# A maximum of three as the third plus two relus kept in PSUM, with the third's product folded into the down sums

## The chip, the cores and the metric

One core of a Trainium2 chip runs the whole program. The metric is the device time of one execution in microseconds (us), the median over several runs. The kernel before: 1981.44 us, median of 3 runs (1980.41 to 1981.76).

## What is computed

Eight batches of 3072 rows with 256 columns go through a real Fourier transform along the rows, a complex 256x256 product with bias, a soft threshold on real and imaginary part, and the inverse transform. The result, 24576 rows of 256, goes through a maxout layer: three products up to 768 columns, their maximum, and one product down to 256.

```python
X = np.fft.rfft(x, axis=1); Xr, Xi = X.real, X.imag
Yr = Xr @ w_r - Xi @ w_i + b_r
Yi = Xr @ w_i + Xi @ w_r + b_i
Yr = np.sign(Yr) * np.maximum(np.abs(Yr) - 0.01, 0.0)   # Yi likewise
y = np.fft.irfft(Yr + 1j * Yi, n=3072, axis=1)          # reshaped to 24576 x 256

h = np.maximum(np.maximum(y @ w1, y @ w2), y @ w3)      # 24576 x 768
out = h @ w_out                                         # 24576 x 256
```

## The kernel before

Products that must be accurate are made of three f16 matmuls: each operand is split into a high and a low f16 part, and `mm3` (lines 178 to 181) issues high x high, high x low and low x high into one PSUM sum. Splitting takes two instructions: ScalarE (ACT) writes the high part, VectorE (DVE) subtracts it and writes the low part (`split_later`, lines 165 to 176, the DVE half handed to `later` and issued at the next `flush`).

The program has a prologue (batch 0's transform, and the maxout weights, which come as float64 bit patterns and are put together and split on DVE and ACT) and then one long loop: batches b (8), chunks c of 384 rows (8 per batch), and units f (6 per chunk, 128 of the 768 up columns each). That makes 64 chunks and 384 units. In a unit:

- `up` (line 1047) makes three products `pu`, i = 0, 1, 2 for w1, w2, w3. Each is two `mm3` (256 = 2 x 128 rows of the weight), so 6 matmuls of 384 columns; a unit has 18. ACT copies the first into SBUF (`c1`, line 1056), DVE takes the maximum with the second in place (line 1059) and with the third into `h32` (line 1062), and `h32` is split into `hh`.
- `down` (line 1071) multiplies `hh` of a unit two units old with its 128 rows of w_out: three groups of 128 rows, each one `mm3`, so 9 matmuls of 256 columns, summed over the six units of a chunk into the two PSUM tiles `pd`. After the sixth, ACT writes them out as `o` (line 1091).

Between these steps of the loop, `run_until(pos)` issues the Fourier work of later batches at positions counted in units (the list `events`), three times per unit: at pos - 2/3, pos - 1/3 and pos. For one block k of that work the path is: `ab`, split by `split_a` and moved across partitions by four DMAs on SP's queue; `stage_b`, 16 matmuls into `px` (line 737); two ACT copies of `px` (`tt` at line 173, `s` at line 750), DVE's low part of `tt` (line 174) and its sum into `s` (line 753), ACT's and DVE's split of `s` (lines 170 and 171); then `stage_w1`, 6 matmuls into `py` that read this last split; then `stage_w2`, 12 more. `stage_w1` is placed one position, one unit, behind `stage_b`. There are 77 such blocks. Each engine takes its instructions in the order in which they stand.

The inverse transform of the next chunk (`inverse`) makes `yh` and `yl`, the split of y.

PSUM has eight banks: three tiles for `pu`, three for all Fourier work, two for `pd`.

Of the kernel before, what the change touches and what calls it, by code (L numbers as in the profile page):

```python
# [101 lines left out]
def fourier_maxout_kernel(  # L102
# [105 lines left out]
    wuh = const.tile([P, 3, KD, FF], F16, name="wuh")  # L208
    wul = const.tile([P, 3, KD, FF], F16, name="wul")
# [18 lines left out]
    def first_homes():  # L228
        g = ga_sb.bitcast(F32).rearrange("p i e n m -> p (i e n m)")
        w = wuh.bitcast(F32).rearrange("p i k f -> p (i k f)")  # L230
        homes = [quad_tile("aq"), quad_tile("aq"), quad_tile("zq")]
        homes += [g[:, i * NQ * D:(i + 1) * NQ * D] for i in range(3)]
        return homes + [w[0:96, i * NQ * D:(i + 1) * NQ * D] for i in range(2)]
# [110 lines left out]
    class Weights:  # L344
        def __init__(self, name, parts):
            self.name, self.parts, self.raw = name, parts, {}
            self.mx = fft.tile([P, len(parts)], F32, name="mw" + name, bufs=1)

        def load(self, n, homes=None):
            width = 2 * self.parts[n][0].shape[1]  # L350
# [17 lines left out]
        def scale(self):  # L368
            e = exponent_of(self.mx, self.name, 20, 0x7FF, 910.0)
            self.e = small("ew" + self.name)  # L370
            nc.vector.tensor_scalar(
                out=self.e, in0=e, scalar1=1.0, scalar2=-896.0, op0=ALU.mult, op1=ALU.add
            )
            self.sc = power("sw" + self.name, e, -1.0, 1164.0, 1)

        def phases(self, n):
            raw = self.raw[n]
            pair, width = raw.shape[1:3]
            if pair == 2:
                hi, lo = self.parts[n][4]  # L380
# [30 lines left out]
            def finish():  # L411
                split_scaled(hi, lo, m, self.sc)

            return exponent, combine, join, finish
# [5 lines left out]
        (wuh[:, i, kd, v:v + HALF], wul[:, i, kd, v:v + HALF], None,  # L420
         up_v[i][:, 2 * v:2 * v + 2 * HALF].rearrange("(k p) w -> p k w", p=P),
         [t[:, i, :, v:v + HALF] for t in (wuh, wul)])
        for v in range(0, FF, HALF) for i in range(3) for kd in range(KD)
    ])
# [6 lines left out]


# [614 lines left out]
    def up(y, f, i):  # L1047
        p = ps.tile([P, 512], F32, name="pu", tag="up", bufs=3)[:, 0:NT]
        for kd in range(KD):
            mm3(  # L1050
                p, wuh[:, i, kd, f * P:(f + 1) * P], wul[:, i, kd, f * P:(f + 1) * P],
                y[0][:, kd], y[1][:, kd], start=kd == 0, stop=kd == KD - 1,
            )
# [18 lines left out]
    def down(b, c, f, hh):  # L1072
        end = b == NB - 1 and c == NCH - 1
        if f == 0:
            st["pd"] = [ps.tile([P, 512], F32, name="pd", tag="dn", bufs=2) for _ in range(2)]
        pd = [st["pd"][t // 2][:, t % 2 * D:t % 2 * D + D] for t in range(3)]
        for t in range(3):
# [3 lines left out]
                stop=f == NF - 1 and t != 0, skip_group_check=t < 2,  # L1081
            )
        if f == NF - 1:
# [52 lines left out]
    for n in range(0, 6, 2):  # L1136
        planned(n, prepare, w_up, n)
        planned(5 + n // 2, phase, w_up, n)
# [13 lines left out]
    for k in range(-3, NJP + 1):  # L1152
        for fn, i in (
            (load_a, k + 3), (stage_b, k + 1), (stage_w, k), (finish_w, k), (stage_q, k - 1),
        ):
            if 0 <= i < NJP:
                if fn == stage_q and i == NJP - 1:
                    total = small("total")
                    nc.vector.tensor_tensor(out=total, in0=w_up.e, in1=w_dn.e, op=ALU.add)
                    st["lim", "u"] = limits("u", total, 273.0)  # L1160
# [55 lines left out]
    behind = []  # L1216
    st["slot"] = 0
    for b in range(NB):
        for c in range(NCH):
            nxt = (b, c + 1) if c + 1 < NCH else (b + 1, 0) if b + 1 < NB else None  # L1220
            for f in range(NF):
                pos = b * SLOTS + c * NF + f
                up(y, f, 0)
# [7 lines left out]
                up(y, f, 1)  # L1231
# [5 lines left out]
                hh = up(y, f, 2)  # L1237
                behind.append((b, c, f, hh))
# [6 lines left out]
                if b == c == 0:  # L1245
                    pumps(5)
                    if f == 2:
                        with tc.issue_after(quiet[0]):
                            split_fft_weights(fft_weights)
                    if f in (3, 5):  # L1250
# [9 lines left out]
            y = y_next  # L1260
    flush()
# [35 lines left out]
```

## Time and profile before

| | |
|---|---|
| median of 3 runs | 1981.44 us |
| span of the profiled execution | 1978.9 us |
| TensorE (PE) busy | 1961.3 us, 99% |
| VectorE (DVE) busy | 1521.3 us, 77% |
| ScalarE (ACT) busy | 1064.3 us, 54% |
| GpSimd (POOL) busy | 280.5 us, 14% |
| main loop starts | at about 110.8 us |

The span runs from the first to the last instruction. The profiled execution's own time is not listed beside it; the three runs stand 1.5 to 2.9 us above the span. A matmul's duration in the trace is from its start to the end of its result; the next one starts long before that, so the time that PE spends on one is the distance from start to start, not the mean duration of its row.

### The profile page before, as it was taken

What the parts mean: (1) busy time and instruction counts of PE and PEld (TensorE: products, weight loads), DVE (VectorE), ACT (ScalarE), POOL (GpSimd) and SP (SyncE); (2) the same over time, 40 slices, a digit from 0 to 9 for tenths busy, and PEclk for the clock granted to TensorE, in tenths of its full rate; (3) what the DMA queues carried; (4) which work ended last, traced back from release to release, by engine and by line L of the source; (5) the groups of instructions that cost most, each with busy time, mean ns of one, the idle gap of its engine ahead of it and who ended that gap; (6) DMA issues with size and microseconds to landing.
All of it is one profiled execution on the core that took longest, in us unless ns stands there. A gap on an engine that the chain in (4) does not pass through costs nothing.

```text
span 1978.9 us, 44328 instructions
## 1 busy us (share of the span) xinstructions
PE 1961.3 (99%) x16839; PEld 1355.9 (69%) x16839; DVE 1521.3 (77%) x3159; ACT 1064.3 (54%) x2186; POOL 280.5 (14%) x510
## 2 busy tenths in 40 slices
PE   9989999999999999999999999999999999999999
PEld 5746776676766766666766676666676677766666
DVE  3788887888877988778887888868887687765554
ACT  5755664566545565456554565545655455443343
POOL 1001111111111122111121021111122001100000
PEclk9999999999999999999999999999999999999999
DMA  8756564565545564555555465544552344221111
GB/s 291 212 150 172 157 163 124 156 174 154 145 133 163 143 189 115 151 150 161 159 137 149 133 186 145 147 139 130 149 154 73 90 115 123 68 76 49 49 49 33
DMA packets 201843, 269.75 MB, mean 136 GB/s; under 512 B 30846, under 2 KB 149982, under 8 KB 201534
## 3 DMA queue, kind: packets, MB, share of 16 engines
q1 hardware_dynamic: 168830, 191.37, 36.7%
q0 software_dynamic: 25168, 68.59, 10.7%
q10 hardware_dynamic: 7632, 6.95, 1.2%
q8 instruction: 133, 2.18, 0.5%
q14 instruction: 80, 0.66, 0.1%
HBM read 124.31 MB, written 75.50 MB: 101 GB/s over the span
## 4 chain that ended last, share of the span: by engine, by line
PE 93%; DVE 3%; DMA 2%; ACT 1%; issue 1%; SPq 0%; ACTq 0%; DVEq 0%
PE pu L179 19%; PE pu L181 18%; PE pu L180 18%; PE pd L181 6%; PE pd L180 6%; PE pd L179 6%; PE py L179 3%; PE py L180 3%; PE py L181 3%; PE pi L1021 2%; PE px L737 2%; PE pa L575 2%; PE pz L905 1%; PE pa L592 1%; PE py L692 0%
## 5 line engine op out<-in xcount | busy, mean ns | idle before, releaser
L179 PE MATMUL pu<-yh,wuh 128*128 128x384 f16 x2304 | 752.2, 327 | 2.6 <-DVE h L1062 1.7
L181 PE MATMUL pu<-yh,wul 128*128 128x384 f16 x2304 | 751.5, 326 | 0.0
L180 PE MATMUL pu<-yl,wuh 128*128 128x384 f16 x2304 | 751.5, 326 | 0.0
L173 ACT ACTIVATE hh<-h 128x384 f16<-128x384 f32 x384 | 200.2, 521 | 432.3 <-DVE h L1062 428.4
L181 PEld LDWEIGHTS <-wul 128*128 128x128 f16 x2304 | 225.5, 98 | 149.7 <-issue 0.9
L179 PEld LDWEIGHTS <-wuh 128*128 128x128 f16 x2304 | 225.3, 98 | 145.1 <-issue 34.2
L181 PE MATMUL pd<-woh,hh 128*128 128x256 f16 x1152 | 313.4, 273 | 0.7 <-DVE hh L174 0.7
L180 PE MATMUL pd<-wol,hh 128*128 128x256 f16 x1152 | 313.8, 273 | 0.0
L179 PE MATMUL pd<-woh,hh 128*128 128x256 f16 x1152 | 313.8, 273 | 0.0
L180 PEld LDWEIGHTS <-wuh 128*128 128x128 f16 x2304 | 225.5, 98 | 116.1 <-issue 5.0
L174 DVE SCALAR_TENSOR_TENSOR hh<-h,hh 128x384 f16<-128x384 f32 x384 | 213.3, 555 | 108.3 <-ACT hh L173 105.4
L1059 DVE TENSOR_TENSOR c<-pu,c 128x384 f32<-128x384 f32 x384 | 212.1, 552 | 95.8 <-PE pu L181 90.3
L1056 ACT ACTIVATE c<-pu 128x384 f32<-128x384 f32 x384 | 186.7, 486 | 139.9 <-PE pu L181 136.8
L1062 DVE TENSOR_TENSOR h<-pu,c 128x384 f32<-128x384 f32 x384 | 211.7, 551 | 29.2 <-PE pu L181 24.8
L1093 POOL DMA_DIRECT2D out_dram<-o x189 | 104.7, 559 | 581.3 <-ACT o L1091 569.7
L585 POOL DMA_DIRECT2D a_d<-aq x160 | 94.0, 591 | 612.4 <-ACT aq L582 590.0
L181 PE MATMUL py<-wch,tt 128*128 128x256 f16 x504 | 137.3, 273 | 0.0
L179 PE MATMUL py<-wch,tt 128*128 128x256 f16 x504 | 137.3, 272 | 0.0
L180 PE MATMUL py<-wcl,tt 128*128 128x256 f16 x504 | 137.3, 272 | 0.0
L179 PEld LDWEIGHTS <-hh 128*128 128x128 f16 x1152 | 112.7, 98 | 33.5
L180 PEld LDWEIGHTS <-hh 128*128 128x128 f16 x1152 | 112.7, 98 | 33.4
L181 PEld LDWEIGHTS <-hh 128*128 128x128 f16 x1152 | 112.7, 98 | 15.2 <-DVE hh L174 1.9
(236 smaller groups left out, 2659.3 us busy)
## 6 DMA issues: line engine op xcount, KB each, us to landing
zq<-z_d SPq DMA_DIRECT2D x63, 384.0 KB, 4.8
out_dram<-o POOLq DMA_DIRECT2D x189, 128.0 KB, 3.3
ab<-a_d SPq DMA_DIRECT2D x84, 256.0 KB, 4.1
ab<-ab SPq DMA_DIRECT2D x336, 64.0 KB, 3.0
vb<-vb SPq DMA_DIRECT2D x308, 64.0 KB, 2.9
z_d<-zs POOLq DMA_DIRECT2D x70, 256.0 KB, 3.8
xm<-in_x_dram SPq DMA_DIRECT2D x40, 384.0 KB, 3.5
a_d<-aq POOLq DMA_DIRECT2D x160, 96.0 KB, 2.9
```

The lines of the kernel that those rows point to most:

```text
L173: nc.scalar.activation(out=hi, in_=src, func=AF.Copy, scale=scale)
L174: later(lambda: low(nc.vector.scalar_tensor_tensor(out=lo, in0=src, scalar=scale, in1=h, op0=ALU.mult, op1=ALU.subtract)))
L179: nc.tensor.matmul(o, lh, rh, start=start, stop=False, **kw)
L180: nc.tensor.matmul(o, lh, rl, start=False, stop=False, **kw)
L181: st["mm"] = nc.tensor.matmul(o, ll, rh, start=False, stop=stop, **kw)
L575: st["mm"] = nc.tensor.matmul(pa[r][64 * h:64 * h + 64], ft[rows, t], xt[rows, i, h], start=t == i, stop=t == 1,)
L585: nc.gpsimd.dma_start(out=av[1 - r, :, :, n:n + 512], in_=o[64 * h:64 * h + 48])
L737: nc.tensor.matmul(pv[:, h, :, g // 2, g % 2], ah[:, g // 2, g % 2, h * P:(h + 1) * P], mb_sb[:, i, 4 * kb + g].rearrange("p (c m) -> p c ...
L1056: st["act"] = nc.scalar.activation(out=c1, in_=p, func=AF.Copy)
L1059: st["dve"] = nc.vector.tensor_tensor(out=c1, in0=p, in1=c1, op=ALU.max)
L1062: st["dve"] = nc.vector.tensor_tensor(out=h32, in0=p, in1=st["c1"], op=ALU.max)
L1093: q.dma_start(out=out_v[b, c, t], in_=o)
```

## The change

max(a, b, c) = c + relu((b - c) + relu(a - b)). The weights are held as W1 - W2 and W2 - W3 (`finish` subtracts the next weight before the split), so `up` has two products. The first, y(W1 - W2), goes into `pu`; ACT applies relu to it in place, in PSUM; the second, y(W2 - W3), is accumulated onto it; DVE then takes max(., 0), scaled, into `h32`. The term c, y W3, is not formed: G = W3 Wout is made once (`turn_last` transposes W3 by matmuls with the identity, `join_last` multiplies it with w_out) and y G joins the down sums: 6 matmuls of 256 columns for each group of 128 rows, at f = 0, 1, 2 of a chunk (in the first chunk all at f = 5). The second product of a unit is issued one unit later, behind the first product of the next unit, and `down` follows that.

```diff
-    wuh = const.tile([P, 3, KD, FF], F16, name="wuh")
+    wuh = const.tile([P, 2, KD, FF], F16, name="wuh")
+    wth = const.tile([P, NF, D], F16, name="wth")
+    gh = const.tile([P, KD, D], F16, name="gh")
...
             def finish():
+                if self.less:
+                    other = self.raw[n + 2][:, :, :, 1].bitcast(F32)
+                    nc.vector.tensor_tensor(out=m, in0=m, in1=other, op=ALU.subtract)
                 split_scaled(hi, lo, m, self.sc)
...
+    def turn_last(n):
+        m = w_up.raw[n][:, :, :, 1].bitcast(F32)
+        first = (n // 6) * (NF // 2)
+        for fs in ((0, 1), (2,)):
+            pt = ff_tile("pw").rearrange("p (f c) -> p f c", c=D)
+            for i, f in enumerate(fs):
+                for kd in range(KD):
+                    nc.tensor.matmul(
+                        pt[:, i, kd * P:(kd + 1) * P], m[:, kd, f * P:(f + 1) * P], id_sb, start=True, stop=True
+                    )
+            to = slice(first + fs[0], first + fs[-1] + 1)
+            split_scaled(wth[:, to], wtl[:, to], pt[:, 0:len(fs)], w_up.sc)
+
+    def join_last():
+        pg = ff_tile("pg").rearrange("p (k d) -> p k d", k=KD)
+        for kd in range(KD):
+            for f in range(NF):
+                mm3(
+                    pg[:, kd], *(t[:, f, kd * P:(kd + 1) * P] for t in (wth, wtl)), woh[:, f], wol[:, f],
+                    start=f == 0, stop=f == NF - 1,
+                )
+        split_scaled(gh, gl, pg, H_SCALE)
...
-    def up(y, f, i):
-        p = ps.tile([P, 512], F32, name="pu", tag="up", bufs=3)[:, 0:NT]
+    def up(y, f, i, p=None):
+        if i == 0:
+            p = ps.tile([P, 512], F32, name="pu", tag="up", bufs=3)[:, 0:NT]
...
         if i == 0:
-            st["c1"] = c1 = ffn.tile([P, NT], F32, name="c1")
-            st["act"] = nc.scalar.activation(out=c1, in_=p, func=AF.Copy)
-        elif i == 1:
-            c1 = st["c1"]
-            st["dve"] = nc.vector.tensor_tensor(out=c1, in0=p, in1=c1, op=ALU.max)
-        else:
-            h32 = ffn.tile([P, NT], F32, name="h32")
-            st["dve"] = nc.vector.tensor_tensor(out=h32, in0=p, in1=st["c1"], op=ALU.max)
-            hh = ffn.tile([P, 2, NT], F16, name="hh", bufs=4)
-            split_later(hh[:, 0], hh[:, 1], h32, H_SCALE)
-            return hh
+            st["act"] = nc.scalar.activation(out=p, in_=p, func=AF.Relu)
+            return p
+        h32 = ffn.tile([P, NT], F32, name="h32")
+        st["dve"] = nc.vector.tensor_scalar(
+            out=h32, in0=p, scalar1=0.0, scalar2=H_SCALE, op0=ALU.max, op1=ALU.mult
+        )
+        hh = ffn.tile([P, 2, NT], F16, name="hh", bufs=4)
+        split_later(hh[:, 0], hh[:, 1], h32)
+        return hh
...
+        for t in range(3):
+            if f == (NF - 1 if first else t):
+                for kd in range(KD):
+                    mm3(
+                        pd[t], *(v[:, kd, t * P:(t + 1) * P] for v in y), gh[:, kd], gl[:, kd],
+                        start=False, stop=first and kd == KD - 1 and t != 0, skip_group_check=t < 2,
+                    )
...
+    def second():
+        b, c, f, y, p = open_unit
+        behind.append((b, c, f, y, up(y, f, 1, p)))
...
-                up(y, f, 0)
+                unit = b, c, f, y, up(y, f, 0)
                 flush()
...
                 run_until(pos - 2 / 3)
-                up(y, f, 1)
+                if open_unit:
+                    second()
+                open_unit = unit
                 flush()
...
-                hh = up(y, f, 2)
-                behind.append((b, c, f, hh))
                 if len(behind) > 2:
                     down(*behind.pop(0))
```

What that does to the order of the engines is shown at three places; the names in the rows are those of the tiles above, and lines are those of the kernel that the row belongs to.

On TensorE, in the middle of the program, the end of a `down` of one of a chunk's first three units and what follows it now:

```order
L181 MATMUL pd<-woh,hh 128x256
L179 LDWEIGHTS yh
L179 MATMUL pd<-gh,yh 128x256
L180 LDWEIGHTS yh
L180 MATMUL pd<-gl,yh 128x256
L181 LDWEIGHTS yl
L181 MATMUL pd<-gh,yl 128x256
```

Before, the next product of `up` stood right behind the row of line 181; now six of these matmuls (two times the three shown) come between in half of the units, and no third product of `up` comes at all.

On VectorE, around one block's split of `px` and of its sum `s` (the 40th of the 77), before:

```order
L174 SCALAR_TENSOR_TENSOR tt<-px,tt 128x2x256
L753 SCALAR_TENSOR_TENSOR s<-px,s 128x256
L1062 TENSOR_TENSOR h_13480<-pu,c_13433 128x384
L171 TENSOR_TENSOR tt<-s,tt 128x2x128
L174 SCALAR_TENSOR_TENSOR hh<-h_13480,hh 128x384
```

and now:

```order
L174 SCALAR_TENSOR_TENSOR tt<-px,tt 128x2x256
L1089 TENSOR_SCALAR h_12377<-pu 128x384
L783 SCALAR_TENSOR_TENSOR s<-px,s 128x256
L171 TENSOR_TENSOR hh<-h_12377,hh 128x384
L171 TENSOR_TENSOR tt<-s,tt 128x2x128
```

The unit's `h` now stands ahead of the sum into `s`, and the low part of `hh` ahead of the low part of the sum, which the matmuls into `py` read; one maximum per unit is gone.

On ScalarE, a stretch of two units of the changed kernel:

```order
L1086 ACTIVATE pu<-pu 128x384
L173 ACTIVATE zh<-zq,s0u 96x1024
L670 ACTIVATE ab<-ab 128x512
L858 ACTIVATE cs<-py,s1x 128x256
L170 ACTIVATE hh<-h_12453 128x384
L1086 ACTIVATE pu<-pu 128x384
L173 ACTIVATE vb<-u,s0v 128x512
L170 ACTIVATE hh<-h_12512 128x384
```

The relu `pu<-pu` of a unit stands ahead of the `hh` of the unit before it, for 379 of the 384 units (for three more it is two ahead); for the other two it stands behind.

## Rows read from the trace of the kernel before

**Rows 1.** The page, parts 1 and 2: span, busy time of TensorE and VectorE, granted clock

```profile
span 1978.9 us, 44328 instructions
PE 1961.3 (99%) x16839; PEld 1355.9 (69%) x16839; DVE 1521.3 (77%) x3159; ACT 1064.3 (54%) x2186; POOL 280.5 (14%) x510
PEclk9999999999999999999999999999999999999999
```

**Rows 2.** The page, part 4: the chain that ended last, by engine

```profile
PE 93%; DVE 3%; DMA 2%; ACT 1%; issue 1%; SPq 0%; ACTq 0%; DVEq 0%
```

**Rows 3.** Waits of TensorE, the main loop's longest: us in total, times, longest us

```profile
PE pu L179 <- DVE h L1062: 1.7, 1, 1.7
PE pd L181 <- DVE hh L174: 0.7, 1, 0.7
PE px L737 <- DMA ab<-ab: 0.2, 1, 0.2
```

**Rows 4.** Timeline of TensorE near the end: start us, duration us; 18 up, 9 down

```profile
1960.72 0.33 PE L179 MATMUL pu<-yh,wuh 128*128 128x384 f16 x1
...
1963.64 0.27 PE L179 MATMUL pd<-woh,hh 128*128 128x256 f16 x1
...
1964.62 0.33 PE L179 MATMUL pu<-yh,wuh 128*128 128x384 f16 x1
```

**Rows 5.** The page, part 5: groups of up and down; busy us, mean ns

```profile
L179 PE MATMUL pu<-yh,wuh 128*128 128x384 f16 x2304 | 752.2, 327 | 2.6 <-DVE h L1062 1.7
L179 PE MATMUL pd<-woh,hh 128*128 128x256 f16 x1152 | 313.8, 273 | 0.0
L179 PEld LDWEIGHTS <-hh 128*128 128x128 f16 x1152 | 112.7, 98 | 33.5
L1059 DVE TENSOR_TENSOR c<-pu,c 128x384 f32<-128x384 f32 x384 | 212.1, 552 | 95.8 <-PE pu L181 90.3
L1056 ACT ACTIVATE c<-pu 128x384 f32<-128x384 f32 x384 | 186.7, 486 | 139.9 <-PE pu L181 136.8
L1062 DVE TENSOR_TENSOR h<-pu,c 128x384 f32<-128x384 f32 x384 | 211.7, 551 | 29.2 <-PE pu L181 24.8
L173 ACT ACTIVATE hh<-h 128x384 f16<-128x384 f32 x384 | 200.2, 521 | 432.3 <-DVE h L1062 428.4
```

**Rows 6.** Groups by line: the f32 matmuls with the identity

```profile
L267 PE MATMUL pt<-id_sb,col 128*128 128x128 f32 (+1 forms) x38 | 7.3, 279 | 0.6 <-DVE col L265 0.6
```

**Rows 7.** The tile pd: VectorE's one scaled read of PSUM (ns, min/median/max)

```profile
L1087 DVE TENSOR_SCALAR o<-pd,s1u x1: 484/484/484, 1974.8 to 1974.8; 128x256 f32<-128x256 f32 x1
```

**Rows 8.** Stretches of the loop: first chunk, the rest (us; busy by engine)

```profile
110.80:140.00 29.20, 26.21 (x169) 14.87 (x169) 27.75 (x56) 14.35 (x28) 0.51 (x1) 0.93 0.50 148
140.00:1971.00 1831.00, 1829.97 (x16200) 1270.59 (x16198) 1429.52 (x2940) 978.17 (x2034) 270.31 (x485) 1.00 0.47 130
```

**Rows 9.** Timeline of one block from px to py: start us, duration us

```profile
732.54 0.63 PE L737 MATMUL px<-mb_all,ab 128*128 128x64 f16 x16
733.00 0.33 PE L179 MATMUL pu<-yh,wuh 128*128 128x384 f16 x1
...
735.49 0.42 ACT L170 ACTIVATE tt<-s 128x256 f16<-128x256 f32 x1 [1.09 <-DVE s L753]
...
735.93 0.42 DVE L171 TENSOR_TENSOR tt<-s,tt 128x256 f16<-128x256 f32 x1
...
736.91 0.27 PE L179 MATMUL py<-wch,tt 128*128 128x256 f16 x1
```

**Rows 10.** Timeline of the next block from px to py

```profile
746.99 0.33 PE L179 MATMUL pu<-yh,wuh 128*128 128x384 f16 x1
...
750.86 0.42 ACT L170 ACTIVATE tt<-s 128x256 f16<-128x256 f32 x1 [1.74 <-DVE s L753]
...
751.31 0.42 DVE L171 TENSOR_TENSOR tt<-s,tt 128x256 f16<-128x256 f32 x1
...
751.77 0.27 PE L179 MATMUL py<-wch,tt 128*128 128x256 f16 x1
```

More of the change, by code (lines that the diff above doesn't have):

```diff
@@ L207, in fourier_maxout_kernel @@
     wcl = const.tile([P, KD, 4, D], F16, name="wcl")
-    wuh = const.tile([P, 3, KD, FF], F16, name="wuh")
-    wul = const.tile([P, 3, KD, FF], F16, name="wul")
+    wuh = const.tile([P, 2, KD, FF], F16, name="wuh")
+    wul = const.tile([P, 2, KD, FF], F16, name="wul")
+    wth = const.tile([P, NF, D], F16, name="wth")
+    wtl = const.tile([P, NF, D], F16, name="wtl")
+    gh = const.tile([P, KD, D], F16, name="gh")
+    gl = const.tile([P, KD, D], F16, name="gl")
     woh = const.tile([P, NF, D], F16, name="woh")
@@ L229, in first_homes @@
         g = ga_sb.bitcast(F32).rearrange("p i e n m -> p (i e n m)")
-        w = wuh.bitcast(F32).rearrange("p i k f -> p (i k f)")
+        both = [w.bitcast(F32).rearrange("p i k f -> p (i k f)") for w in (wuh, wul)]
         homes = [quad_tile("aq"), quad_tile("aq"), quad_tile("zq")]
         homes += [g[:, i * NQ * D:(i + 1) * NQ * D] for i in range(3)]
-        return homes + [w[0:96, i * NQ * D:(i + 1) * NQ * D] for i in range(2)]
+        return homes + [w[0:96, 0:NQ * D] for w in both]
     def load_fft_weights():
@@ L344, in fourier_maxout_kernel, with __init__ @@
     class Weights:
-        def __init__(self, name, parts):
-            self.name, self.parts, self.raw = name, parts, {}
+        def __init__(self, name, parts, less=False):
+            self.name, self.parts, self.raw, self.less = name, parts, {}, less
             self.mx = fft.tile([P, len(parts)], F32, name="mw" + name, bufs=1)
         def load(self, n, homes=None):
-            width = 2 * self.parts[n][0].shape[1]
+            width = self.parts[n][3].shape[2] if self.parts[n][3] is not None else self.parts[n][2].shape[1]
             if homes:
@@ L373, in scale @@
             )
-            self.sc = power("sw" + self.name, e, -1.0, 1164.0, 1)
+            self.sc = power("sw" + self.name, e, -1.0, 1163.0, 1)
         def phases(self, n):
@@ L419, in fourier_maxout_kernel @@
     w_up = Weights("u", [
-        (wuh[:, i, kd, v:v + HALF], wul[:, i, kd, v:v + HALF], None,
+        (None, None, None,
          up_v[i][:, 2 * v:2 * v + 2 * HALF].rearrange("(k p) w -> p k w", p=P),
-         [t[:, i, :, v:v + HALF] for t in (wuh, wul)])
+         [t[:, i, :, v:v + HALF] for t in (wuh, wul)] if i < 2 else None)
         for v in range(0, FF, HALF) for i in range(3) for kd in range(KD)
-    ])
+    ], less=True)
     w_dn = Weights("d", [
@@ L1080, in down @@
                 pd[t], lh, ll, woh[:, f], wol[:, f], start=f == 0 and t != 1,
-                stop=f == NF - 1 and t != 0, skip_group_check=t < 2,
+                stop=f == NF - 1 and not first and t != 0, skip_group_check=t < 2,
             )
+        for t in range(3):
[5 more added lines that the diff above has]
+                    )
         if f == NF - 1:
@@ L1159, in fourier_maxout_kernel @@
                     nc.vector.tensor_tensor(out=total, in0=w_up.e, in1=w_dn.e, op=ALU.add)
-                    st["lim", "u"] = limits("u", total, 273.0)
+                    st["lim", "u"] = limits("u", total, 271.0)
                 fn(i)
@@ L1249, in fourier_maxout_kernel @@
                             split_fft_weights(fft_weights)
+                    if f == 4:
+                        turn_last(10)
+                    if f == 5:
+                        join_last()
                     if f in (3, 5):
@@ L1260, in fourier_maxout_kernel @@
             y = y_next
+    second()
+    flush()
     flush()
```

14 lines of the change are left out of this document (9 added, 5 removed).

## The prediction

> **What bounds the kernel now.** I read the page first: TensorE is busy for 99% of the span at full granted clock, VectorE for 77%, ScalarE for 54% [rows 1], and the chain that ended last lies on TensorE for 93% [rows 2]. Busy time alone would not settle it, since a matmul's row reaches to the end of its result and neighbours overlap. So I looked for what TensorE waits for: in the main loop the longest waits are 1.7, 0.7 and 0.2 us, each once [rows 3]. Then I read the distance from start to start. In the last chunk 18 up matmuls stand in 1963.64 - 1960.72 = 2.92 us, 162.2 ns each, and the 9 down matmuls behind them in 0.98 us, 108.9 ns each [rows 4], where the mean durations are 327 and 273 ns [rows 5]. TensorE is a full pipe, and its time is the number of matmuls times these distances. What a change takes out of it comes off the span, as long as nothing else becomes late.
>
> **What goes and what comes on TensorE.** The third product of every unit goes: 384 units x 6 = 2304 matmuls of 384 columns, x 162.2 ns = 373.7 us. y G comes: 64 chunks x 18 = 1152 matmuls of 256 columns, of the shape of the down matmuls and with a weight load each like them, x 108.9 ns = 125.4 us. G is made once: 36 matmuls of 256 columns, 3.9 us, and 12 f32 transposes, each two records in the trace. No row gives their distance. The nearest group, f32 with the identity, lasts 279 ns [rows 6], so 24 x 0.279 = 6.7 us at most, and 1.3 us if each takes half of a 256-column step; I take 24 x 0.109 = 2.6 us. Sum: -373.7 + 125.4 + 3.9 + 2.6 = -241.8 us.
>
> The price of a matmul by its columns is where the Trainium skill speaks against this change. The rows show 162 and 109 ns in a stream in which every matmul has its own weight load. The page "TensorE: Matmul & The Clock Gate", section "Back-to-back issue gap", gives for such a stream about 81 ns at 128 columns and 131 ns at 512; read off between these (an estimate), the removed matmuls would cost 114 ns and the added ones 98 ns, and the sum would be about -144 us instead of -242 us. The rows disagree with that figure, and the rows decide; the same section's formula for a single matmul's gap, columns / 2.4 + 2.5 ns, gives 162.5 and 109.2 ns and agrees with them.
>
> **ScalarE.** The copy of the first product (486 ns [rows 5]) becomes a relu in place. No row of before shows ScalarE writing PSUM. The nearest rows are that copy, same source and shape, and the 521 ns of `hh`; I take 486 ns, so ScalarE's load stays. The new wait is the second product's for this relu. Ahead of it, after the unit's own first product, TensorE has six matmuls of the unit before, a down of nine or fifteen and the next unit's six: 6 x 0.162 + 9 x 0.109 + 6 x 0.162 = 2.9 us at least, against 0.33 - 0.16 us for the last matmul to end and 0.49 us for the relu, 0.65 us. Cost nothing, with 2.3 us to spare; without that cover 0.65 us per unit.
>
> **VectorE.** One maximum per unit goes (212.1 us in all [rows 5]); the other becomes one instruction with a single input from PSUM. The nearest rows are 551 ns, same source and shape [rows 5], and the one scaled read of PSUM, 484 ns for 256 columns [rows 7], which by columns would be 726 ns; I take 551 ns. The low part of `hh` keeps its shape. Per pair of weights there is a subtraction more (four in all), two final splits are gone, five splits for G come: a few us in total. VectorE ends at about 1521 - 212 + 5 = 1314 us, ScalarE near 1067 us; neither can be the bound. In the loop VectorE's share stays, (1429.5 - 212) / (1831 - 242) = 77% against 78%, and ScalarE's rises from 53% to 62% [rows 8]. `pu` has three tiles as before, and a tile is now free two units after it was taken, which is hidden. The DMAs of the loop are the same ones, in 12% less time; TensorE waited for such a transfer once, 0.2 us [rows 3].
>
> **The first chunk** is different. There VectorE is busy for 27.75 of 29.20 us [rows 8] with the last weights. Its work changes by 6 x -0.55 us for the maxima; two subtractions less one split (768 columns each) and the splits of the transposes and of G (512, 256 and 512) are 2048 columns more, 2.9 us at the 551 ns per 384 columns of [rows 5]; TensorE's by 36 x -0.162 + 5.2 us of transposes and G. Both are within 1 us of nothing, so the sum above holds. In G, TensorE must wait for both splits of the second half's transposes, behind other VectorE work: I give it 2 us.
>
> **What is late next.** The Fourier work is placed by units, and a unit becomes shorter by six up matmuls, 0.97 us, and longer by six down matmuls in half of them. Its chains between engines don't shrink by themselves. The tightest is from `px` to `py`. In the one block `py` starts 736.91 - 733.00 = 3.91 us after the last `px` matmul: 18 up and 9 down. ScalarE's part of the last split is there 2.91 us after it, VectorE's 3.35 us [rows 9]. The order of the changed kernel has 12 up and 9 down there, 2.93 us, and the third matmul, which reads VectorE's part, starts 0.22 us later: 0.20 us late. In the next block `py` stood 4.78 us behind `px`, and VectorE's part was done at 4.74 us, 0.26 us before the third matmul [rows 10]; now the distance falls by 0.97 us and VectorE's queue by one maximum, 0.55 us, so it is about 0.16 us late. In the order, `h` and the low part of `hh` moreover stand ahead of the block's sum now. Of 77 such blocks 16 have the 2.93 us. I take 0.2 us each, 15 us, and 3 us for transfers that come late in the same way. The ends are nothing (no block late) and 0.97 us each, 75 us (no chain any shorter).
>
> **Sum.** -241.8 + 2 + 15 + 3 = -222 us. The span goes from 1978.9 to 1757 us. The profiled execution's own time isn't given; the median of the runs is 1981.44 us, 2.5 us above the span, and with the same 2.5 us the time is **1759 us**.
>
> **Rivals.**
> - *The chains set the pace.* The waits that I put at 20 us are most of the 75 us, or more with the transfers. For it: in rows 10 the chain ended 0.04 us before `py`, and three engines in a row with a queue each rarely get shorter. Against it: VectorE's share doesn't rise, and its order holds one instruction less per unit. Time: 1740 + 75 = 1815 us.
> - *The relu is on the path, and it is slower than before.* The place is ScalarE's queue: `hh` waits there for VectorE, 428.4 us over the kernel [rows 5], and a relu that stands behind it waits too, and the second product with it. Paid in full, 0.65 us x 384 = 250 us: 1759 + 250 = 2009 us. It decides from 222 / 384 = 0.58 us per unit. Against it: the order has the relu ahead of the earlier unit's `hh` for 382 of 384 units, and TensorE has 2.9 us of other work in between.
> - *Matmuls are paced by their weight loads, not their columns.* A load takes 98 ns [rows 5], nearly the 109 ns of a 256-column matmul. If only the number of loads counted, 2304 - 1152 - 36 - 24 = 1092 fewer at 98 ns would give 107 us: 1981 - 107 + 20 = 1894 us. Against it: the 384-column matmuls stand 162 ns apart with the same loads [rows 4]. [...]
>
> That the change doesn't do what it says can be left out: the order has 4608 up matmuls where 6912 were, and 1152 more into `pd`.
>
> **How the numbers follow.** My forecast (TensorE bound, waits from nothing to 50 us, 1740 to 1790 us) gets 0.82; the chains 0.13; the relu 0.03; the loads 0.02. The range takes in the forecast, down to the lower end of the transposes' price, and most of the chains: 1738 to 1808 us. Runs of this kernel can tell 0.2%, 4 us, from no change. Every case but the relu is faster by far more, and the relu paid in part can land near nothing: faster 0.97, the same 0.01, slower 0.02.
>
> **What would show it.** In the profile after, up and down matmuls should still stand 162 and 109 ns apart, with 4608 and 4608 records. TensorE should remain above 97% busy, VectorE near 1314 us. Waits of TensorE should name VectorE's `tt` or ScalarE's `tt` at `py`, 0.1 to 0.5 us each, and none of note for ScalarE's `pu`. If waits add up to over 50 us, the second step (what is late next) is wrong; if the distances differ, the first one; if `pu` waits for the relu, the ScalarE part.

## The result, and the profile after

| | before | after |
|---|---|---|
| median | 1981.6 us (4 runs, 1980.41 to 1982.7) | **1794.55 us** (4 runs, 1785.19 to 1799.37) |
| profiled execution, its span | not listed, 1978.9 us | 1798.86 us, 1797.1 us |

The ratio is 0.9051, with a 95% interval of 0.9022 to 0.908: 187 us less. That lies inside the predicted range of 1738 to 1808 us, 36 us above the predicted 1759 us and 5 us above the forecast's own range of 1740 to 1790 us. Without any wait the prediction's price of -241.8 us would give 1739.8 us. So the question of this part is where some **55 us** went. The profiled execution is one of the longer ones, 4.3 us above the median.

The page of the kernel after, its parts 1, 2 and 4 and groups of part 5:

```profile
PE 1743.3 (97%) x15747; PEld 1254.6 (70%) x15747; DVE 1335.1 (74%) x2782; ACT 1060.0 (59%) x2189; POOL 283.9 (16%) x510
...
PE 65%; DVE 17%; DMA 9%; ACT 5%; issue 2%; SPq 2%; ACTq 0%; DVEq 0%
...
L179 PE MATMUL pu<-yh,wuh 128*128 128x384 f16 x1536 | 502.5, 327 | 4.8 <-DVE h L1089 4.0
L170 ACT ACTIVATE hh<-h 128x384 f16<-128x384 f32 x384 | 199.8, 520 | 242.1 <-DVE h L1089 231.5
L179 PE MATMUL pd<-woh,hh 128*128 128x256 f16 x1152 | 315.0, 273 | 3.7 <-ACT o L1128 3.2
L1086 ACT ACTIVATE pu<-pu 128x384 f32<-128x384 f32 x384 | 184.4, 480 | 190.5 <-PE pu L181 188.7
L1089 DVE TENSOR_SCALAR h<-pu 128x384 f32<-128x384 f32 x384 | 212.0, 552 | 101.1 <-PE pu L181 100.0
```

Against [rows 1, 2, 5]: TensorE issues 1092 matmuls fewer and its share falls from 99% to 97%; the chain that ended last lies on TensorE for 65% where it was 93%; of the other 28 points VectorE got 14, the DMAs 7, ScalarE 4. The new instructions have the durations that were taken for them: the relu in PSUM 480 ns (486 were taken), the maximum with zero 552 ns (551). The spacing holds too. The timeline of TensorE near the end (start us, duration us): 12 up matmuls in 1.95 us, 162.5 ns each, then 9 down matmuls in 0.98 us, 108.9 ns each, as in [rows 4].

```profile
1774.86 0.33 PE L179 MATMUL pu<-yh,wuh 128*128 128x384 f16 x1
...
1776.81 0.27 PE L179 MATMUL pd<-woh,hh 128*128 128x256 f16 x1
...
1777.79 0.33 PE L179 MATMUL pu<-yh,wuh 128*128 128x384 f16 x1
```

What is new are waits of TensorE (us in total, times, longest us), where [rows 3] had three of 2.6 us together in the main loop:

```profile
PE px L767 <- DMA ab<-ab: 11.4, 22, 1.3
PE pi L1051 <- DMA ze<-zl: 6.8, 9, 1.9
PE pu L179 <- DVE h L1089: 4.0, 2, 3.1
...
PE pz L935 <- DMA vb<-vb: 3.5, 4, 1.9
PE pd L179 <- ACT o L1128: 3.2, 6, 1.8
...
PE py L179 <- DVE y L1065: 2.2, 1, 2.2
...
PE pu L179 <- ACT pu L1086: 0.5, 1, 0.5
```

They stand mostly at matmuls that read what a DMA brought (`px`, `pi`, `pz`: 21.7 us). At `py`, where the prediction put 15 us, there is one wait of 2.2 us in the loop, for VectorE's `y`, and none for `tt`. TensorE waits 0.5 us for the relu.

The windows of the kernel after show when (us; busy time of PE, PEld, DVE, ACT, POOL, granted clock, DMA share, GB/s): from 140 to 1755 us TensorE sat idle for 1615 - 1580.4 = 34.6 us, where before it had 1.0 us in 1831 [rows 8]; in the first chunk its granted clock was 0.81.

```profile
112.60:140.00 27.40, 21.78 (x138) 12.71 (x138) 26.21 (x52) 13.87 (x27) 0.00 (x0) 0.81 0.51 146
140.00:1755.00 1615.00, 1580.38 (x14848) 1144.70 (x14847) 1228.36 (x2535) 961.05 (x2008) 270.81 (x480) 1.00 0.55 146
```

Idle time alone misses short delays inside the pipe, so I also added up TensorE's time from start to start over all matmuls, by the tile they write. "Price" is before with the prediction's counts (`pu` at two thirds of its 1133.2 us, which takes 377.7 us off where 162.2 ns a matmul gave 373.7); the last column is the best version of the experiments below.

| us, by tile written | before | price | after | best version |
|---|---|---|---|---|
| `pu` (up) | 1133.2 | 755.5 | 773.6 | 763.7 |
| `pd` (down, with y G) | 381.3 | 506.7 | 512.6 | 510.0 |
| `px` | 51.9 | 51.9 | 60.6 | 55.1 |
| `pi` (inverse) | 54.4 | 54.4 | 66.6 | 59.3 |
| `pz` | 45.6 | 45.6 | 54.8 | 50.3 |
| `pa` | 76.0 | 76.0 | 81.4 | 78.0 |
| `py` | 214.2 | 214.2 | 213.6 | 215.1 |
| the rest | 16.4 | 22.9 | 28.1 | 24.8 |
| sum | 1973.0 | 1727.2 | 1791.0 | 1756.4 |

The profiled execution is 63.8 us above this price: it is a longer one, and this price is 4 us lower. A matmul's time here runs to the start of the next one, so a wait is counted with the matmul ahead of the one that waits. Counted with the one that waits, `px` rose from 63.2 to 79.7 us, `pi` from 70.8 to 80.8, `pz` from 43.1 to 51.0, `pa` from 65.8 to 72.5 and `py` from 216.1 to 220.5. So the loss is spread over all Fourier stages, and `py` has 4.4 us of it.

### The profile page after: what moved, and what is told of

Read it like the earlier page. It is cut to its first block, busy times and chain, and to the rows that moved or that the text cites. A ratio compares the mean times of both kernels' runs of the same rounds, so it can differ in the third digit from the quotient of the medians.

```text
span 1797.1 us, 41168 instructions
## 1 busy us (share of the span) xinstructions
PE 1743.3 (97%) x15747; PEld 1254.6 (70%) x15747; DVE 1335.1 (74%) x2782; ACT 1060.0 (59%) x2189; POOL 283.9 (16%) x510
## 3 DMA queue, kind: packets, MB, share of 16 engines
q8 instruction: 125, 2.05, 0.5%
## 4 chain that ended last, share of the span: by engine, by line
PE 65%; DVE 17%; DMA 9%; ACT 5%; issue 2%; SPq 2%; ACTq 0%; DVEq 0%
PE pu L179 10%; PE pu L180 9%; PE pu L181 9%; PE pd L179 7%; PE pd L180 6%; PE pd L181 6%; DMA ab<-ab 3%; PE py L179 2%; PE pi L1051 2%; PE py L181 2%; PE py L180 2%; DVE h L1089 2%; PE px L767 2%; DMA zq<-z_d 1%; DVE hh L171 1%
## 5 line engine op out<-in xcount | busy, mean ns | idle before, releaser
L179 PE MATMUL pu<-yh,wuh 128*128 128x384 f16 x1536 | 502.5, 327 | 4.8 <-DVE h L1089 4.0
L180 PE MATMUL pu<-yl,wuh 128*128 128x384 f16 x1536 | 501.9, 327 | 0.1
L181 PE MATMUL pu<-yh,wul 128*128 128x384 f16 x1536 | 502.0, 327 | 0.0
L1086 ACT ACTIVATE pu<-pu 128x384 f32<-128x384 f32 x384 | 184.4, 480 | 190.5 <-PE pu L181 188.7
L1089 DVE TENSOR_SCALAR h<-pu 128x384 f32<-128x384 f32 x384 | 212.0, 552 | 101.1 <-PE pu L181 100.0
L171 DVE TENSOR_TENSOR hh<-h,hh 128x384 f16<-128x384 f32 x384 | 212.7, 554 | 82.1 <-ACT hh L170 81.5
L181 PEld LDWEIGHTS <-wul 128*128 128x128 f16 x1536 | 150.6, 98 | 101.0 <-issue 2.3
L179 PEld LDWEIGHTS <-wuh 128*128 128x128 f16 x1536 | 150.4, 98 | 93.2 <-issue 22.8
L180 PEld LDWEIGHTS <-wuh 128*128 128x128 f16 x1536 | 150.6, 98 | 77.5 <-issue 7.2
L1065 DVE SCALAR_TENSOR_TENSOR y<-pi,ye 128x192 f32<-128x192 f32 x252 | 111.2, 505 | 27.6 <-ACT ye L1059 27.6
```

Source lines behind the costliest of these rows:

```text
L171: later(lambda: nc.vector.tensor_tensor(out=lo, in0=src, in1=h, op=ALU.subtract))
L179: nc.tensor.matmul(o, lh, rh, start=start, stop=False, **kw)
L180: nc.tensor.matmul(o, lh, rl, start=False, stop=False, **kw)
L181: st["mm"] = nc.tensor.matmul(o, ll, rh, start=False, stop=stop, **kw)
L1065: nc.vector.scalar_tensor_tensor(out=yv[:, e], in0=pv[:, 0], scalar=(1 - 2 * e) * Y_SCALE, in1=ev, op0=ALU.mult, op1=ALU.add,)
L1086: st["act"] = nc.scalar.activation(out=p, in_=p, func=AF.Relu)
```

## The experiments

**The theory** after this view: the price is right, and the loss is waits that arise because the Fourier work is placed in units and a unit became shorter, while splits and transfers did not. Rivals: the new instructions themselves (the relu on ScalarE, the order on VectorE) are in the way; or the loss is the disturbed first chunk and its half clock.

**1. Units as long as before.** The first product of each unit is computed twice, so that TensorE has its 2304 matmuls back, and all else is the change.

```diff
-        for kd in range(KD):
+        for kd in [n for _ in range(2 - i) for n in range(KD)]:
```

> The first product of every unit is computed twice into the same tile: 2304 matmuls of 384 columns come back, so a unit is as long as before plus y G, all other instructions as in the changed kernel. Price alone: 1794.6 + 2304 x 0.1622 = 2168 us. Theory A: with the old unit length the waits in the loop go, 35 to 55 us, so 2113 to 2133 us. Theory D (the waits belong to the new order: relu in place, second product a unit later, y G): they stay, 2155 to 2170 us.

Measured: 2109.17 us (2107.47 to 2114.54), ratio 1.0644 [1.0622, 1.0667], 4 us below the range of theory A and far from that of D. The price says 1739.8 + 373.7 = 2113.5 us without any wait. From after to here it is 314.6 us and not 373.7: 59 us of waits are gone, the waits for `ab`, `ze` at 1051 and `vb` are no longer among the longest, and from 140 to 2060 us TensorE sat idle for 0.55 us (window, then waits):

```profile
140.00:2060.00 1920.00, 1919.45 (x17073) 1358.95 (x17074) 1250.74 (x2539) 979.20 (x2010) 275.44 (x480) 1.00 0.46 123
```

```profile
PE pi L179 <- ACT zh L173: 2.6, 1, 2.6
PE pz L748 <- DVE mxu L733: 2.1, 1, 2.1
PE pt L271 <- DVE col L269: 1.9, 2, 1.6
```

So the price holds to 4.3 us, and the whole loss comes with the shorter unit. The new instructions, all of them still in this kernel, cost nothing that shows by being there. What this can't tell apart is why a shorter unit costs: the leads counted in units shrink, and every other engine and queue has the same work in less time. Experiments 4 to 10 go at that.

**2. The relu.** It is applied to 16 of the 384 columns and left out on the others, so the output isn't the layer's.

```diff
-            st["act"] = nc.scalar.activation(out=p, in_=p, func=AF.Relu)
+            st["act"] = nc.scalar.activation(out=p[:, 0:16], in_=p[:, 0:16], func=AF.Relu)
```

> The relu in PSUM is applied to 16 of the 384 columns of each first product only, the rest is left without it: ScalarE loses some 100 to 130 us of work, and the second product's wait is as good as gone. If the relu is on TensorE's path: 20 us or more less. If ScalarE's queue makes the chains late (theory E2): 15 to 40 us less, 1755 to 1780 us. Theory A and the prediction's ScalarE part: within 8 us of 1794.

Measured: 1788.76 us (1784.48 to 1794.47), ratio 0.9034 [0.9012, 0.9056], ScalarE busy 951.1 us in place of 1060.0. That is 6 us less with overlapping intervals, from 109 us less work. The relu is not on the path.

**3. The first chunk.** Its splits of the Fourier weights are moved from the third to the sixth unit.

```diff
-                    if f == 2:
+                    if f == 5:
                         with tc.issue_after(quiet[0]):
                             split_fft_weights(fft_weights)
```

> The split of the Fourier weights (a run of some 5 us on VectorE in the first chunk) is issued at the chunk's sixth unit, not at its third. Theory A for the first chunk (this run holds up h, and so the up products that need its tile): TensorE's wait of 3.05 us for h near 131 us and the fall of the clock from 133 to 140 us go, time 5 to 9 us less, 1786 to 1790 us. Rival: VectorE has the same work in the chunk, so the wait only moves, time within 3 us of 1794.

Measured: 1790.44 us (1789.41 to 1794.31), ratio 0.9036 [0.9022, 0.905], between the two expectations. In the kernel after, TensorE waited 3.05 us for `h` in the first chunk, whose turn on VectorE came behind those splits (timeline of VectorE, start us, duration us), and then ran at half clock from 133.2 to 140.0 us:

```profile
129.94 1.27 DVE L137 SCALAR_TENSOR_TENSOR wcl<-wst,sc,wch 128x256 f16<-128x256 f32 x3
...
132.40 0.87 DVE L137 SCALAR_TENSOR_TENSOR wcl<-wst,sc,wch 128x256 f16<-128x256 f32 x2
...
134.12 0.54 DVE L1089 TENSOR_SCALAR h<-pu 128x384 f32<-128x384 f32 x1
```

That stretch of half clock is gone here, and 0.9 us are left of the wait; the waits in the loop are much the same. 4 us, less than the kernel's own spread: a small part at most.

**4. One transfer earlier.** `split_a`, which makes `ab`, is placed 0.8 units earlier.

```diff
-                (0, load_a, k + 3), (-0.8, split_a, k + 1), (1.6, finish_w, k - 1), (1, stage_b, k + 1),
+                (0, load_a, k + 3), (-1.6, split_a, k + 1), (1.6, finish_w, k - 1), (1, stage_b, k + 1),
```

> The split and the moves of each block's input are issued 0.8 units earlier (position -1.6 for -0.8), nothing else. Theory A (units got shorter, so transfers that are placed by units land too late): TensorE's waits at px for the moves (11.4 us in 22 waits in the changed kernel) fall below 3 us, and the time to 1775 to 1786 us. Theory B (the moves are late because SP's queue or the memory is too busy for the shorter time): issuing them earlier doesn't help, px waits stay near 11 us and the time within 5 us of 1794. Theory C (the chains over VectorE and ScalarE from px to py, as in the prediction): no change in time, waits at py decide.

Measured: 1792.62 us (1790.22 to 1796.27), ratio 0.9045 [0.903, 0.906]. The wait that was aimed at is gone, as theory A has it, but the time is that of theory B: others grew. Waits of TensorE:

```profile
PE pz L935 <- DMA vb<-vb: 8.4, 10, 1.6
PE pi L1051 <- DMA ze<-zl: 7.1, 9, 2.3
PE pd L179 <- ACT o L1128: 5.7, 6, 1.8
```

A likely reading, not tested by itself: the wait at `px` had been giving the chains behind it time that they now lack.

**5. Another transfer earlier.** The loads of `zq` come two units earlier and their split one.

```diff
-                if nxt and f == (2 if late else 1):
+                if nxt and f == (2 if b == c == 0 else 1 if late else 0):
...
-                if ahead and f == 5:
+                if ahead and f == 3:
```

> The load of z is issued two units earlier and its split and moves one unit earlier (first chunk unchanged). Theory A: TensorE's waits at pi for ze (6.8 us in 9 waits, up to 1.9 us) fall below 2 us, the second fall of the clock near 345 us goes, time 1780 to 1788 us. Theory B: waits at pi stay, or others at px grow by as much, time within 5 us of 1794.

Measured: 1817.13 us (1815.59 to 1818.81), ratio 0.9168 [0.9154, 0.9181], 23 us worse. The wait for `ze` fell from 6.8 to 5.6 us, and those for `ab` (11.4 to 12.8), `vb` (3.5 to 10.3) and `xhl` (1.8 to 7.7) rose. `py` waits 4.4 us for `s`. Neither theory allowed for that. It may be that what is put earlier in a queue makes what stood there later; which queue that would be was not tried.

**6. All of a block's chain earlier.** Experiments 3 and 4 together, all steps of a block (from batch 2 on) 1.5 units earlier, and `stage_q`, whose matmuls read `vb`, 0.7 units later in its block.

```diff
-            p = 8 + 2.13 * (k + 2) if b == 1 else (b - 1) * SLOTS + 2.72 * (k + 2)
+            p = 8 + 2.13 * (k + 2) if b == 1 else (b - 1) * SLOTS + 2.72 * (k + 2) - 1.5
...
-                (3.2, stage_q, k - 1), (2, stage_w, k), (2.4, stage_w2, k),
+                (3.9, stage_q, k - 1), (2, stage_w, k), (2.4, stage_w2, k),
```

> Placing by units redone for the shorter unit: input moves 0.8 units earlier, the blocks of batches 2 to 7 start 1.5 units earlier, stage_q 0.7 units later behind its moves, the split of the Fourier weights at the first chunk's sixth unit. Theory A (the lost time is lateness of chains that are placed by units): TensorE's waits at px, pz and pi (11.4, 3.5 and 6.8 us named in the changed kernel) together fall below 8 us and the time to 1755 to 1780 us. Theory E (a queue between them has no room left, so a wait removed at one place comes back at the next, as from px to pz in the run with early moves): above 1785 us.

Measured: 1771.2 us (1769.94 to 1773.32), ratio 0.8943 [0.8928, 0.8958]: 23 us gained by places alone (some 4 of them by experiment 3), with every instruction the same. Waits for transfers are down to 2.3 and 3.1 us, and `py` now waits, for VectorE's `y` and ScalarE's `zs`:

```profile
PE py L179 <- DVE y L1065: 4.3, 5, 1.1
PE pa L605 <- DVE xhl L174: 4.1, 8, 0.6
PE pi L1051 <- DMA ze<-zl: 3.1, 5, 0.9
...
PE py L179 <- ACT zs L941: 2.6, 5, 0.9
PE pz L748 <- DVE mxu L733: 2.5, 1, 2.5
PE px L767 <- DMA ab<-ab: 2.3, 3, 1.3
```

**7. The queues.** SP's waits for `xhl` had grown from 117.9 to 162.2 us, so in one kernel GpSimd issues the loads of x in SP's place:

```diff
-                        nc.sync.dma_start(out=xn[r:r + n], in_=xv[0:n])
+                        nc.gpsimd.dma_start(out=xn[r:r + n], in_=xv[0:n])
...
-            nc.sync.dma_start(out=xm.rearrange("p (n d) -> p n d", n=NQ), in_=xv)
+            nc.gpsimd.dma_start(out=xm.rearrange("p (n d) -> p n d", n=NQ), in_=xv)
```

> The loads of x in the loop are issued by GpSimd, no longer by SP, where they wait for free tiles ahead of the moves between partitions. Theory E1 (SP's queue is what makes moves late): waits at px, pz and pi fall by more than half, 1760 to 1780 us. If the lateness comes from VectorE or ScalarE: within 6 us of 1794.

Measured: 1835.06 us (1831.1 to 1839.88), ratio 0.9267 [0.9246, 0.9288], 41 us worse, a case that the expectation did not have. TensorE waits 25.7 us for `ze`. GpSimd's waits suggest the way: its loads now wait for their buffers ahead of its stores of `z_d`, which `ze` is made from. The wait of `z_d` itself is not new, it was 216.7 us in the kernel after:

```profile
POOL xm L540 <- DVE mxx L545: 235.1, 33, 17.4
POOL z_d L944 <- ACT zs L941: 205.3, 34, 23.7
...
POOL xq L516 <- DVE xhl L174: 75.1, 15, 11.9
```

SP's queue did not become free by this: its waits for `vb` rose from 72.7 to 239.0 us. So the run does not decide whether SP's queue makes the transfers late.

In the other kernel VectorE's queue is made shorter: the low part of `hh` is left out. The matmuls that read it read the high part instead, which so counts twice, and the output is far from the layer's.

```diff
-        split_later(hh[:, 0], hh[:, 1], h32)
+        nc.scalar.activation(out=hh[:, 0], in_=h32, func=AF.Copy)
...
-            lh, ll = (hh[:, i, t * P:(t + 1) * P] for i in range(2))
+            lh, ll = (hh[:, 0, t * P:(t + 1) * P] for i in range(2))
```

> The low part of hh is left out; the down matmuls that read it read the high part instead, so TensorE has the same matmuls, and VectorE loses 213 us of work (384 instructions of 554 ns). Theory E3 (VectorE's queue, 80% busy in the loop, makes the chains and the moves behind them late): waits fall by half or more, 1745 to 1770 us. If it is not VectorE: within 8 us of 1794.

Measured: 1771.59 us (1766.81 to 1773.76), ratio 0.8942 [0.8925, 0.8959], 1.6 us above the range of theory E3. 23 us are gained although VectorE was busy for only 74% of the span (76% of the loop): its queue has a part in the lost time. The waits for `ab`, `ze` and `vb` fell from 21.7 to 13.1 us.

**8. Do the two gains add?** Experiment 6 with the low part left out as in 7 (the high part counts twice here too; "less exact" in the expectation is too mild).

> The version with the block's steps shifted earlier (1771 us), and the low part of `hh` left out (the third of a down product's matmuls reads the high part again, so TensorE has the same work and the output is less exact). If the two are different shares of the lost 55 to 60 us, the steps being placed too late and VectorE's queue being too long, their gains add: 1771 - 23 = 1748 us. If both remove the same waits, the time is 1765 to 1771 us. The matmuls' own price gives 1737 us as the floor.

Measured: 1755.59 us (1752.38 to 1759.27), ratio 0.885 [0.8835, 0.8864]. On top of experiment 6 it is 15.6 us in place of 23 by the times; by the ratios, each to the kernel before on the same chip, it is 18 in place of 22. So most of the gain adds, and not all of it: places and queue are two handles on waits that are in part the same.

**9. The low part on GpSimd.** Experiment 6, and GpSimd subtracts it.

```diff
-        split_later(hh[:, 0], hh[:, 1], h32)
+        nc.scalar.activation(out=hh[:, 0], in_=h32, func=AF.Copy)
+        later(lambda: nc.gpsimd.tensor_tensor(out=hh[:, 1], in0=h32, in1=hh[:, 0], op=ALU.subtract))
```

> The version with the block's steps shifted earlier (1771 us), and the low part of `hh` is subtracted by GpSimd in place of VectorE, 384 instructions. Leaving it out on VectorE alone gave 23 us from 1794.6. If VectorE's queue is what delays the transfers, the time falls here to 1750 to 1762 us. If GpSimd is too slow at it or takes VectorE's turn at the memory, `pd` waits for `hh` and the time is 1780 us or more.

Measured: 1776.23 us (1772.67 to 1776.82), ratio 0.8955 [0.8942, 0.8969]: between the two expectations, and no gain on experiment 6, where leaving the part out gives 15.6 us. The 5 us between the times are not clear of noise: the intervals of the two ratios overlap. GpSimd is not too slow for it (1095 ns each, and TensorE does not wait for it by name):

```profile
L1094 POOL TENSOR_TENSOR hh<-h,hh 128x384 f16<-128x384 f32 x384 | 420.5, 1095 | 862.3 <-ACT hh L1093 860.7
```

But VectorE is busy for 1196.2 us where leaving the part out gave 1157.0, in the same places (experiment 8): the same 2398 instructions took 39 us more. Which ones is told in the last section.

**10. `py` later behind `px`.** Experiment 6, with the two parts of the last products 0.34 and 0.3 units later.

```diff
-                (3.9, stage_q, k - 1), (2, stage_w, k), (2.4, stage_w2, k),
+                (3.9, stage_q, k - 1), (2.34, stage_w, k), (2.7, stage_w2, k),
```

> The version with the block's steps shifted earlier (1771 us) with one thing more: the first and second half of the block's last products, `py`, stand 0.34 and 0.3 units later behind `px`. If the waits that this version still has at `py` (4.3 us for `y`, 2.6 us for `zs`) are the chain from `px` to `py` being shorter than before, as the prediction had it, they fall by some 5 us and the time to about 1765 us. If the loss is shared by all queues, the wait moves to what reads the result of `py` later, `zq` and its transfers, and the time stays at 1770 to 1775 us.

Measured: **1764.49 us** (1764.39 to 1767.89), ratio 0.8904 [0.8891, 0.8917], the best version that computes all: 30 us below the change as given, 25 above the price. The waits at `py` are gone and the time is the expected one, in part by luck. In the two profiled executions the first `pu` starts at 115.69 us in experiment 6 and at 111.45 us here (timelines of TensorE), so 4.2 of the 8.0 us between their spans lie ahead of the loop, where both kernels have the same instructions.

```profile
115.69 0.80 PE L179 MATMUL pu<-yh,wuh 128*128 128x384 f16 x2 [0.26 <-ACT yh L173]
```

```profile
111.45 0.80 PE L179 MATMUL pu<-yh,wuh 128*128 128x384 f16 x2 [0.26 <-ACT yh L173]
```

Nor does the reason hold that this expectation lent the waits. They named `y`, which reads `pi`, and `zs`, which reads `pz`; neither feeds `py`. All Fourier work shares three PSUM tiles, so what `py` waited for there was, by these names, a tile to become free.

**11. Whose `tt` does `py` read?** The prediction's late step rested on `py` reading the split of the `px` ahead of it. The instructions with their tiles' numbers, kernel before, TensorE, then VectorE:

```
3424 L737 MATMUL px_3717<-mb_all_77,ab_3251 128x2x32
3480 L179 MATMUL py_3805<-wch_79,tt_3521 128x256
3684 L179 MATMUL py_3989<-wch_79,tt_3734 128x256

471 L174 SCALAR_TENSOR_TENSOR tt_3521<-px_3504,tt_3521 128x2x256
493 L174 SCALAR_TENSOR_TENSOR tt_3734<-px_3717,tt_3734 128x4x128
```

The `py` next behind `px_3717` reads the split of `px_3504`, one block earlier. The list of places says the same, `(1, stage_b, k + 1)` beside `(2, stage_w, k)`: the unit between the two steps lies between different blocks. The test on the chip puts `py` 0.9 units earlier, right behind that wrong `px`:

```diff
-                (3.2, stage_q, k - 1), (2, stage_w, k), (2.4, stage_w2, k),
+                (3.2, stage_q, k - 1), (1.1, stage_w, k), (1.5, stage_w2, k),
```

> The change as it is, with one thing moved: the products `py` of a block 0.9 units (about 4 us) earlier, so that they stand right behind the `px` that the prediction took for theirs, in place of about a unit behind it. If the prediction read the chain rightly (that `px` is the one whose split `py` reads, ready 3.0 to 5.6 us after it), TensorE must now wait 3 us or more for `tt` in nearly all of 77 blocks: over 200 us more, 2000 us, and the waits name `tt`. If `py` reads the split of the `px` one block before, as the names with their numbers in the order say (in the changed kernel its third matmul starts 6.4 us or more after that split's low part is done), 2 us of that are left at the least, no wait for `tt` shows, and the time is within 1780 to 1805 us.

Measured: 1801.68 us (1799.62 to 1803.87), ratio 0.9092 [0.9077, 0.9107]. No wait names `tt`; TensorE's waits at `py` are 3.8, 2.3 and 0.6 us, the first for `s`, which reads `px`, the others as in experiment 10:

```profile
PE px L767 <- DMA ab<-ab: 18.0, 26, 2.2
...
PE py L179 <- DVE s L783: 3.8, 4, 1.0
...
PE py L179 <- ACT zs L941: 2.3, 3, 1.1
```

The reading by the numbers is the right one. From the starts and ends of all 77 blocks: the third `py` matmul starts at least 8.5 us after its own low part is done in the kernel before, 6.4 us after the change, and still 3.8 us in this one.

## Why the prediction was right, and the step that failed

- **TensorE as a full pipe, and its price: right.** The spacings held, G's 36 matmuls took 3.9 us as predicted, and experiment 1 meets the price to 4.3 us. The transposes are 4.2 us from start to start in the best version, where 2.6 were taken, between the bounds of 1.3 and 6.7 (7.6 us in the kernel after, with the 3.05 us wait behind them). The rival that weight loads set the pace is out. The Trainium skill, "TensorE: Matmul & The Clock Gate", section "Back-to-back issue gap", would by its figures for pairs of load and matmul have given -144 us (the prediction's estimate); the measured -187 us is more than that even with all waits inside, so the trace and the time speak for the same section's formula instead.
- **ScalarE and VectorE: right.** The relu takes 480 ns and TensorE waited 0.5 us for it. VectorE is busy for 1335 us where 1314 were predicted: 212 us of maxima are gone, but busy time counts overlapping neighbours once, so it fell by 186 us.
- **First chunk: small, as predicted.** The wait of 2 us in G did not come: its 36 matmuls take 3.9 us with no wait. The 3.05 us for `h` came instead, and moving the splits that delayed `h` gave 4 us, within the spread. Half clock in the whole execution is 20.7 us, before 9.0, which is worth at most half of the difference, 5.9 us.
- **"What is late next": the failed step.** Two things were wrong in it. First, its chain was not one: the `px` and the `py` of [rows 9, 10] belong to different blocks (experiment 11), and the true chain has 6 us to spare. For the 15 us placed there no wait for `tt` was measured. Second, transfers "that come late in the same way" got 3 us, on the strength of one wait of 0.2 us before; TensorE's waits for them were 21.7 us by name, the largest part of its idle time in the loop. That the loss comes with the shorter unit was right (experiment 1); the place was wrong, and the sum of 20 us measured 55. By the prediction's own sign, waits of over 50 us, it is this step that is wrong.
- **The range held partly by luck.** The time lies above the forecast's 1740 to 1790 us, in the part of the range that stands for the rival of the chains. That rival's 75 us are 77 blocks x 0.97 us on the chain that has 6 us to spare.

A chain that should have been read ends at `px`: `ab` is split on ScalarE and VectorE, goes out in four DMAs on SP's queue and must have landed. Over all 84 blocks, from the trace's starts and ends (mean us of each piece, and the tenth percentile of the last):

| | before | after |
|---|---|---|
| ScalarE's split starts, to VectorE's done | 1.92 | 1.99 |
| to the last of four DMA issues | 1.85 | 2.05 |
| from there to `px` | 5.78 | 4.36 |
| the same, tenth percentile | 3.38 | 2.14 |
| whole | 9.55 | 8.40 |

Such a DMA lands 3.0 us after its issue (median, before and after). Before, nine tenths of the blocks had 3.38 us or more, and 3 of 84 less than 3.0; the change took 1.15 us from the whole and none from the splits and issues, and 18 of 84 came to lie below 3.0 us. That is the subtraction the prediction should have made, and it could have been made from the trace of before: 1.8 units between split and use, each of them 241.8 / 384 = 0.63 us shorter by the price, 1.13 us. It covers the 11.4 us of waits at `px`; that `pi` and `pz` lose in the same way is likely and was not added up. One such wait, kernel after, SP's queue and then TensorE (start us, duration us): the last two of four DMAs go out at 232.6 us, behind one of `vb`, 1.2 us after VectorE finished at 231.4 us; `px` starts at 234.68 us.

```profile
230.55 1.29 SPq L678 DMA_DIRECT2D ab<-ab  x2
231.89 0.60 SPq L894 DMA_DIRECT2D vb<-vb  x1
232.58 1.24 SPq L678 DMA_DIRECT2D ab<-ab  x2
```

```profile
234.68 0.29 PE L767 MATMUL px<-mb_all,ab 128*128 128x64 f16 x4 [0.35 <-DMA ab<-ab]
```

What is shown: the loss comes with the shorter unit (experiment 1), and moving places alone brings back 30 of the 55 us (experiments 6 and 10, with the 4 us ahead of the loop said there). What stays open: the 25 us that the best version is above the price. It idles for 1615 - 1599.6 = 15.4 us from 140 to 1755 us; the rest is short delays and the first chunk, and no experiment took them apart. Nor was it settled why earlier `z` loads cost 23 us, or how much of the loss is short leads and how much is the queues having less time.

```profile
112.60:140.00 27.40, 24.38 (x190) 16.53 (x189) 26.23 (x53) 14.15 (x28) 0.00 (x0) 0.96 0.46 135
140.00:1755.00 1615.00, 1599.55 (x15077) 1165.44 (x15075) 1239.05 (x2560) 977.74 (x2037) 274.23 (x486) 1.00 0.56 147
```

## What to carry to other kernels

Where side work is placed in units of the main work, a cut in the main work is a cut in every lead that was counted in units: list the leads, take the cut from each, compare with the splits, the issues and the landing, and move the places in the same change. Here that gave some 30 us beyond the change itself. A chain between engines is read by the numbers of its tiles, not by the next instruction of the right name. And a wait that is removed alone can turn up at the next chain: in experiments 4 and 5 one move alone gained nothing, and in 6 several together gained 23 us.

## What the runs showed of the hardware

- GpSimd slowed VectorE. With GpSimd subtracting 384 tiles (experiment 9), VectorE's instructions that read two operands from SBUF took longer than in experiment 8, where VectorE has the same instructions and GpSimd none of that work: `yl` 593 ns in place of 556, `vb` 818 in place of 750. The maximum that reads only PSUM stayed at 552 ns (553), and `y`, with one operand in PSUM, at 507. `zl`, which also reads two operands from SBUF, did not change (1281 and 1279 ns); why was not tried. `t`, with one operand, in SBUF, took 462 ns in the mean in place of 429; its median stayed at 426, and single ones took up to 1132 where 496 was the most. Four rows of experiment 9, then two of 8:

```profile
L1089 DVE TENSOR_SCALAR h<-pu 128x384 f32<-128x384 f32 x384 | 212.0, 552 | 207.7 <-PE pu L181 206.0 <-POOL hh L1094 0.8
L1065 DVE SCALAR_TENSOR_TENSOR y<-pi,ye 128x192 f32<-128x192 f32 x252 | 108.9, 507 | 55.2 <-ACT ye L1059 55.1
L1071 DVE TENSOR_TENSOR yl<-y,yh 128x384 f16<-128x384 f32 x126 | 74.8, 593 | 45.5 <-ACT yh L1069 44.8
L174 DVE SCALAR_TENSOR_TENSOR vb<-u,s0v,vb 128x512 f16<-128x512 f32 x84 | 68.7, 818 | 27.2 <-ACT vb L173 26.9
```

```profile
L1071 DVE TENSOR_TENSOR yl<-y,yh 128x384 f16<-128x384 f32 x126 | 70.0, 556 | 45.6 <-ACT yh L1069 44.8
L174 DVE SCALAR_TENSOR_TENSOR vb<-u,s0v,vb 128x512 f16<-128x512 f32 x84 | 63.0, 750 | 27.7 <-ACT vb L173 27.4
```

The Trainium skill, "GPSIMD Engine Reference", section "1. Specifications", says that GpSimd's way to SBUF is shared with VectorE and that they contend where a VectorE instruction has two SBUF inputs; this trace agrees for `yl` and `vb`, and not for `zl`.
- ScalarE writing its result back into PSUM took 480 ns, the copy of the same shape to SBUF before took 486 [rows 5].
- The same transfer landed later in the denser program: `ab<-a_d` 5.3 us after its issue, before 4.1 (medians), with the DMA engines' share at 0.55 in place of 0.47 [rows 8]; before, then after:

```profile
ab<-a_d SPq DMA_DIRECT2D x84, 256.0 KB, 4.1
```

```profile
ab<-a_d SPq DMA_DIRECT2D x84, 256.0 KB, 5.3
```
